# Another order of batch 1's norm beside chunk 0, four transfers on GpSimd's queue, and two sums of w_out elsewhere in chunk 1

## The chip, the core and the metric

The kernel runs on one core of a Trainium2 chip. A core has five engines that run their own instruction queues and wait for one another by semaphores: TensorE (PE, matmuls; PEld is its weight load), VectorE (DVE), ScalarE (ACT), GpSimd (POOL) and SyncE (SP), which here only issues DMA transfers. ScalarE and GpSimd issue transfers too. An engine takes its instructions strictly in order, so that one that waits holds all behind it. The metric is the device time of one execution in microseconds (us), and of several runs the median.

## What is computed

Eight batches of eight heads go through a linear attention with an RMS norm, and the result, seen as 4608 tokens of 512, through a gated feed-forward layer of 1536. All of it is float32; the weights arrive as float64.

```python
def _attn_ref(q, k, v, g_norm):            # q, k, v: (8, 8, 576, 64)
    kv = np.einsum('bhsd,bhse->bhde', k, v)
    out = np.einsum('bhsd,bhde->bhse', q, kv)
    rms = np.sqrt(np.mean(out * out, axis=-1, keepdims=True) + 1e-06)
    return (out / rms * g_norm).astype(np.float32)

def _moe_ref(x, w_gate, w_val, w_out):     # x: (4608, 512), w_gate, w_val: (512, 1536), w_out: (1536, 512)
    gate = 1.0 / (1.0 + np.exp(-(x @ w_gate)))
    val = x @ w_val
    return (gate * val @ w_out).astype(np.float32)
```

## The kernel before

The 4608 tokens are worked in nine chunks of 512. The attention of batch b is put between the matmuls of the chunks ahead of the one that needs it, and its loads further ahead still. Three stretches matter here.

**Chunk 0 (22 to 116 us), first layer.** It is done plainly: eleven blocks of eight matmuls of 512 columns (function `plain`, L599; the profile shows each such matmul as two). A block has a gate (a sigmoid on ScalarE, L604) and an end (a product on VectorE, L607), which are put out beside the next block. Beside each matmul stands a place, numbered 0 to 87, and the string `places` (L807) says which steps are put out there, in which order. Since every engine works in order, this string sets the order of VectorE's and ScalarE's queues. The steps:

- `CV`: the next step of the conversion of the weights from float64 (`convert`, L179). A unit is 128 x 1024 weights; units 0 to 11 are pairs of w_gate and w_val blocks, units 12 to 17 pairs of rows of w_out. It takes five steps on VectorE, L197, L212, L224, L228 and L235 (L237 for w_out), with two of ScalarE between (L202 after the first, L217 after the second). L224 waits for L202, and L228 for L217. When a unit is done its buffer is loaded again, for the unit three further on (L161, L163, on SP). What is left of the steps when the 88 places are over goes beside chunk 0's second layer (L876).
- `a...` and `b...`: the first and second half (`heads_run`, L416) of batch 1's heads: `u` (matmuls, L439), `sq` (square, ScalarE, L444), `s0`, `s1` (reductions, VectorE, L447), `rt` (root, ScalarE, L450, with a load of its function table), `rc` (reciprocal, VectorE, L483), `n0` to `n2` (six scalings each, ScalarE, L479), `x0`, `x1` (two transposes each, VectorE, L462 and L464, and four transfers to xT, SP, L473).
- `t00` to `t11`: transposes of q (VectorE, L408 and L410). `t11` also puts out the twelve loads of batch 2's first q (L119, L120).
- `LL`, `LL2`: the loads of k and v of batches 1 and 2 (`load_late`, L125): eight transfers of 256 KB on SP (L134), and four of 64 KB for the last 64 rows (L139).
- `KV`, `KV2`: the matmuls k times v of batches 1 and 2 (L389, and L396 for the last 64 rows); `C` and `D` copy the results (ScalarE, L404, L405), `ASIDE` sets batch 2's aside (ScalarE, L400).
- `W0`, `W1`: sums of the converted weights on GpSimd (L751).

**Chunk 0, second layer (116 to 158 us).** Twelve rows of w_out in pairs, sixteen matmuls in the profile to a pair (`second`, L833). Pair f needs unit 12 + f/2.

**Chunks 1 to 8.** Both layers go by a scheme with 26 products in place of 32: sums of weights and sums of tokens are multiplied (L957 in the first layer, L1059 in the second), and what comes out is combined on ScalarE (L923) and VectorE (L927). A chunk's first layer has three blocks of 26 products, 0 to 77 in all; its second layer has 26, in the order of `PRODUCTS2` but for a few. GpSimd makes most of the sums of the first layer's results (L733). In chunk 1 the sums of the converted weights are made on the way: of w_gate and w_val, which SP stores for the later chunks (`keep_w1`, L768), and of w_out (`w_form`, L1027). A list at L1151 says which sum of w_out is put out after which product: triples of product, number of the sum, and 1 for GpSimd or 0 for VectorE; `at1` is for the first layer, `at2` counts the products done in the second. Sum 22 (weights 7 and 12) is read by product 10, sum 23 (6 and 14) by product 16. Sum 22 is written over part of the second block's sums of w_gate and w_val, sum 23 over part of the third block's. Both are kept on the core or stored as before.

Behind each second layer stands `load_late` for the batch two chunks on: batch 3's after chunk 1, read at L389 near 282 us.

Of the kernel before, what the change touches and what calls it, by code (L numbers as in the profile page):

```python
# [20 lines left out]
def kernel(  # L21
# [11 lines left out]
    nc = tc.nc  # L33

    B, H, S, HD = q.shape
# [9 lines left out]
    PH = P // 2  # L45
# [19 lines left out]
    GH = G // 2  # L65
# [59 lines left out]
    def load_late(b):  # L125


        if b >= B:
            return
        mains = {}  # L130
        for n in range(NHP):
            for name, src in (("k", k), ("v", v)):
                mains[n, name] = t = kv_place(len(mains))
                nc.sync.dma_start(out=t.rearrange("p (h c) -> p h c", h=2),  # L134
                                  in_=src[b, 2 * n:2 * n + 2, 0:S4].rearrange("h (p j) d -> p h (j d)", j=NK4))
        rest = kv_place(len(mains))
        for i, src in enumerate((k, v)):
            for r in range(2):
                (nc.sync if b == 1 else nc.scalar).dma_start(out=rest[PH * r:PH * r + PH, GH * i:GH * i + GH].rearrange("p (h d) -> p h d", d=HD),  # L139
                                  in_=src[b, NHP * r:NHP * r + NHP, S4:S].rearrange("h p d -> p h d"))  # L140
        kv_late[b] = mains, rest

# [381 lines left out]
    def kv_place(i):  # L524
        return h_more.rearrange("p j s c -> p (j s c)")[:, G * i:G * i + G]
# [256 lines left out]
    def w1_form(c, j, part, v):  # L782
        if c == 1:
# [11 lines left out]
    spare_sg = sgs.pop()  # L795
    batch1, second_batch = feed(1), feed(2)
    named = {"LL": lambda: load_late(1), "LL2": lambda: load_late(2), "KV": batch1[0][0], "KV2": second_batch[0][0],
             "W0": lambda: w1_sums(0), "W1": lambda: w1_sums(1),
             "ASIDE": second_batch[0][2], "CV": convert_step}
# [4 lines left out]
    for i, which in enumerate("ab"):  # L804
# [2 lines left out]
    places = """  # L807
        1:CV,CV 2:CV,Q0 4:CV,CV 5:CV,CV 6:CV,LL 7:CV,CV 10:CV,CV 11:Q1 15:CV 16:CV,CV 17:t00
        18:CV,CV 19:t01 20:KV 22:CV,CV,C 25:CV 26:CV,CV 29:au,LL2 30:CV
        31:asq 32:CV,t10,as0 34:CV,as1,art 35:CV 36:t11,arc,an0 37:an1 38:CV,an2 40:CV,CV 41:CV,ax0  # L810
        43:ax1 44:KV2,ASIDE 46:CV,W0 47:bu 48:CV,CV,bsq 50:CV,bs0 52:CV,CV 54:bs1 55:CV,CV,brt,D 57:CV,CV 58:CV 60:CV,brc
        62:bn0,bn1 63:bn2 64:CV 65:CV,CV,CV 66:CV,CV 67:CV 71:bx0 72:CV 74:W1 75:bx1
        80:CV,CV,CV,CV,CV 84:CV 87:CV,CV
    """
    at_place = {}
    for some in places.split():
        p, names = some.split(":")
# [45 lines left out]
    def x_sum(c, n):  # L863
        if c not in x_ops:
            x_ops[c] = x_sums(c)
        x_ops[c][n]()
# [160 lines left out]
    def w_form(v, eng, at_once=True):  # L1027
        sx_, x, sy, y = next(s_[1:] for s_ in W_SUMS if s_[0] == v)
        if sx_ > 0:
            eng.tensor_tensor(out=W_AT[v], in0=W_AT[x], in1=W_AT[y], op=op_of(sy))  # L1030
        else:
            nc.vector.scalar_tensor_tensor(out=W_AT[v], in0=W_AT[x], scalar=-1.0, in1=W_AT[y], op0=ALU.mult,
                                           op1=op_of(sy))
        if v not in STAY:
            stores.append(lambda: nc.sync.dma_start(out=kept3[STREAM.index(v)].rearrange("p (j n) -> p j n", j=N3),
                                                    in_=W_AT[v]))
            if at_once:
                stores.pop()()

    def second_layer_fast(c, at):  # L1040
# [62 lines left out]
        for i in range(1, NPR):  # L1103
            if i != 3:
# [8 lines left out]
                else:  # L1113
                    product(i, blocks)
                    finish(i)
        load_late(c + 2)

    fill.extend(x_early)
# [13 lines left out]
    for c in range(1, NG):  # L1132
        at1, at2 = {}, {}
        for p, step in x_late:
            at1.setdefault(p, []).append(step)
        x_late = []
        if c + 1 < B:
            kv, first_, then = second_batch if c == 1 else feed(c + 1)
            for p, step in (list(zip((21, 22) if c == 2 else (19, 20), kv)) if c > 1 else []) + first_:
                at1.setdefault(p, []).append(step)  # L1140
            for p, step in zip((3, 6) if c == 1 else (4, 6), then):
                at2.setdefault(p, []).append(step)
        if c + 1 < NG:
            for n, p in enumerate(X1 if c == 1 else X2 if c + 1 < B else X3):
                step = lambda n=n, c=c: x_sum(c + 1, n)
                if p < NPR:
                    at2.setdefault(p, []).append(step)
                else:
                    x_late.append((p - NPR, step))
        if c == 1:  # L1150
            for at_, forms in ((at1, ((28, 9, 0), (30, 10, 0), (34, 12, 0), (52, 11, 1), (57, 14, 0), (58, 8, 1), (61, 19, 0), (64, 16, 1))), (at2, ((1, 13, 0), (2, 22, 0), (3, 23, 1), (4, 25, 1), (9, 15, 0), (10, 24, 0), (10, 20, 0), (11, 17, 0), (12, 18, 0), (13, 21, 0)))):  # L1151
                for p, n, pool_ in forms:
                    at_.setdefault(p, []).append(lambda n=n, eng=nc.gpsimd if pool_ else nc.vector, at_once=at_ is at1 or n == 13: w_form(n, eng, at_once))
        first_layer_fast(c, at1)
        if c == 1:
            sgs += [spare_sg] + more_sgs
        second_layer_fast(c, at2)
# [30 lines left out]
```

## Time and profile before

Three runs: median 1004.05 us (1003.74 to 1005.06). The profiled execution took 1004.44 us, with a span of 1002.7 us from its first to its last instruction.

| engine | busy us | share of the span | instructions |
|---|---|---|---|
| TensorE matmul | 993.8 | 99% | 5958 |
| TensorE weight load | 815.8 | 81% | 5958 |
| VectorE | 722.1 | 72% | 1198 |
| ScalarE | 342.5 | 34% | 606 |
| GpSimd | 617.5 | 62% | 988 |

By stretch, busy us of each engine:

| us | TensorE | VectorE | ScalarE | GpSimd |
|---|---|---|---|---|
| 50 to 75 | 25.00 | 20.20 | 16.43 | 0.00 |
| 75 to 100 | 25.00 | 23.99 | 17.06 | 24.30 |
| 100 to 125 | 24.43 | 24.80 | 9.10 | 24.61 |
| 125 to 150 | 24.84 | 24.57 | 8.49 | 23.74 |
| 230 to 240 | 10.00 | 9.77 | 2.23 | 7.36 |
| 240 to 250 | 10.00 | 9.59 | 1.12 | 9.61 |
| 250 to 260 | 9.67 | 6.79 | 0.00 | 8.24 |
| 300 to 400 | 100.00 | 70.01 | 30.89 | 56.97 |

A line of the timeline gives start and duration in us, the engine, the line of the kernel, the operation, what it writes and reads, how many such instructions in a row, and in brackets how long the engine had been idle before and what ended that. Matmuls are pipelined: each shows longer than the distance to the next one, so that the distance of their starts tells the pace.

### The profile page before, as it was taken

To read this page: it belongs to the slowest core of one execution; us is meant where nothing else is said; L and a number is where in the kernel's file an instruction comes from. 1 tells how busy PE (TensorE), PEld (TensorE's weight loads), DVE (VectorE), ACT (ScalarE), POOL (GpSimd) and SP (SyncE) were. 2 spreads that over 40 slices of the span, in tenths; PEclk is the share of its full clock that TensorE was granted. 3 is DMA by queue.
4 is the path that set the end of the run, shared out by engine and by line. 5 is a ranking of instruction groups with operands and counts; after the bars stand their busy time and mean duration, and the time that the engine had idled before them with its cause. 6 is when DMAs were issued, how large, how long until landed. Compare 5 with 4: busy or idle time off the path is not lost.

```text
span 1002.7 us, 16624 instructions
## 1 busy us (share of the span) xinstructions
PE 993.8 (99%) x5958; PEld 815.8 (81%) x5958; DVE 722.1 (72%) x1198; ACT 342.5 (34%) x606; POOL 617.5 (62%) x988
## 2 busy tenths in 40 slices
PE   8999999999999999999999999999999999999998
PEld 7455447888888888888888888888888888888887
DVE  4989999889757756784677676866587566755672
ACT  4566332562144213530344124421342133213320
POOL 1509997798359633965186707861595449744963
PEclk9999999999999999999999999999999999999999
DMA  9995414673799568846875577755864555444514
GB/s 271 269 265 183 172 51 115 215 236 127 248 301 272 176 189 240 239 156 203 257 240 171 181 223 237 203 171 179 258 201 141 167 173 211 156 149 162 214 53 122
DMA packets 156114, 195.43 MB, mean 195 GB/s; under 512 B 84832, under 2 KB 128864, under 8 KB 156032
## 3 DMA queue, kind: packets, MB, share of 16 engines
q0 software_dynamic: 22000, 114.11, 34.4%
q1 hardware_dynamic: 126864, 78.16, 27.6%
q10 hardware_dynamic: 7168, 2.10, 0.9%
q8 instruction: 47, 0.77, 0.3%
q14 instruction: 35, 0.29, 0.1%
HBM read 160.50 MB, written 25.56 MB: 186 GB/s over the span
## 4 chain that ended last, share of the span: by engine, by line
PE 73%; POOL 2%; DMA 1%; issue 0%; SPq 0%; DVE 0%; POOLq 0%
PE mm L957 46%; PE mm L1059 24%; PE at L439 1%; POOL h L733 1%; PE at L389 1%; DMA h_more<-in_v_dram 1%; POOL w_ring L1030 0%; POOL h_more L733 0%; PE at L396 0%; SPq L134 0%; POOL w L780 0%; DVE sg L927 0%; POOLq L780 0%; POOLq L1030 0%
## 5 line engine op out<-in xcount | busy, mean ns | idle before, releaser
L957 PE MATMUL mm<-xs,w 128*128 128x256 f32 x1428 | 331.8, 380 | 0.0
L957 PEld LDWEIGHTS mm<-xs,w 128*128 128x128 f32 x1428 | 270.5, 190 | 37.1
L957 PE MATMUL mm<-xT,w 128*128 128x256 f32 x948 | 229.8, 380 | 0.0
L957 PEld LDWEIGHTS mm<-xT,w 128*128 128x128 f32 x948 | 179.5, 190 | 25.0 <-issue 0.5
L780 POOL DMA_DIRECT2D w<-kept x84 | 46.8, 557 | 189.4 <-PE mm L957 187.3
L927 DVE TENSOR_TENSOR sg<-sg,mm 128x512 f32<-128x512 f32 (+1 forms) x176 | 100.7, 599 | 85.5 <-PE mm L957 41.5
L1059 PE MATMUL mm<-w,h 128*128 128x256 f32 x630 | 143.1, 379 | 0.3 <-POOL h L733 0.3
L1059 PEld LDWEIGHTS mm<-w,h 128*128 128x128 f32 x630 | 119.6, 190 | 17.0 <-POOL h L733 0.7
L919 POOL TENSOR_TENSOR h<-h,sg 128x512 f32<-128x512 f32 x72 | 96.0, 1350 | 57.0 <-DVE h L927 31.0
L923 ACT COPY temps<-mm 128x512 f32<-128x512 f32 (+1 forms) x128 | 66.0, 538 | 186.9 <-PE mm L1059 94.7
L733 POOL TENSOR_TENSOR h<-h 128x128 f32<-128x128 f32 x216 | 112.1, 531 | 16.6 <-DVE h_more L733 13.1
L1059 PE MATMUL mm<-w,h_more 128*128 128x256 f32 x474 | 108.2, 379 | 0.0
L916 ACT ACTIVATE sg<-sg 128x512 f32<-128x512 f32 x96 | 59.7, 630 | 131.5 <-DVE sg L927 131.5
L1059 PEld LDWEIGHTS mm<-w,h_more 128*128 128x128 f32 x474 | 90.1, 190 | 12.2
L923 ACT COPY sg<-mm 128x512 f32<-128x512 f32 (+1 forms) x112 | 56.9, 510 | 86.5 <-PE mm L1059 45.0
L733 POOL TENSOR_TENSOR h_more<-h 128x128 f32<-128x128 f32 x120 | 61.6, 517 | 34.3 <-DVE h L919 30.0
L927 DVE TENSOR_TENSOR temps<-temps,mm 128x512 f32<-128x512 f32 (+1 forms) x96 | 59.4, 619 | 25.9 <-PE mm L1059 16.6
L599 PE MATMUL mm<-xT,w 128*128 128x512 f32 x176 | 77.8, 596 | 0.1
L927 DVE TENSOR_TENSOR temps<-mm,temps 128x512 f32<-128x512 f32 (+1 forms) x64 | 39.8, 622 | 50.9 <-PE mm L1059 23.6
L923 ACT COPY h<-mm 128x512 f32<-128x512 f32 x48 | 28.1, 585 | 140.4 <-PE mm L957 126.4
L927 DVE TENSOR_TENSOR sg<-mm,sg 128x512 f32<-128x512 f32 (+1 forms) x64 | 39.7, 620 | 45.1 <-PE mm L957 24.5
L599 PEld LDWEIGHTS mm<-xT,w 128*128 128x128 f32 x176 | 32.6, 190 | 39.2 <-issue 36.8
(145 smaller groups left out, 1284.2 us busy)
## 6 DMA issues: line engine op xcount, KB each, us to landing
w<-kept POOLq DMA_DIRECT2D x42, 896.0 KB, 5.7
w<-kept POOLq DMA_DIRECT2D x90, 384.0 KB, 4.6
w<-kept POOLq DMA_DIRECT2D x42, 768.0 KB, 5.5
out_dram<-sg SPq DMA_DIRECT2D x119, 64.0 KB, 1.7
h_more<-in_k_dram SPq DMA_DIRECT2D x28, 256.0 KB, 5.6
h_more<-in_v_dram SPq DMA_DIRECT2D x28, 256.0 KB, 6.5
q<-in_q_dram SPq DMA_DIRECT2D x96, 72.0 KB, 5.0
xT<-xTs SPq DMA_DIRECT2D x96, 72.0 KB, 4.4
```

Of the source, the lines that this page charges most:

```text
L389: nc.tensor.matmul(ps[HD * g:HD * g + HD, m, e], mains[2 * m + g, "k"][:, c], mains[2 * m + g, "v"][:, c], start=(e == 0 and j == 0), stop ...
L439: nc.tensor.matmul(u[HD * e:HD * e + HD, o:o + HD], qTs[HD * g:HD * g + HD, c:c + HD], kvq[HD * g:HD * g + HD, t == NSL, m, e], start=True ...
L599: nc.tensor.matmul(self.ps[i], w[("wg", "wv")[i], self.f][:, m, :], xT[self.c][:, m, :], start=(m == 0), stop=(m == NMT - 1), skip_group_c ...
L733: ops.append((eng, lambda v=v, x=x, sign=sign, y=y, eng=eng: eng.tensor_tensor(out=h_form(v, j), in0=h_form(x, j), in1=h_form(y, j), op=op ...
L780: nc.gpsimd.dma_start(out=granule(g)[:, 0:n], in_=kept1[g // NPA % N3, g % NPA][:, 0:n])
L916: nc.scalar.activation(out=o["o" + step[1]], in_=o["o" + step[1]], func=AF.Sigmoid)
L919: mult.tensor_tensor(out=o[x], in0=o[x], in1=o[y], op=ALU.mult)
L923: nc.scalar.copy(out=o[out_], in_=o[expr])
L927: tt(out=o[out_], in0=o[x], in1=o[y], op=ALU.add if sign == "+" else ALU.subtract)
L957: nc.tensor.matmul(regions[name][1][:, g], ws[:, g], xf[c][wv], start=(new and g == 0), stop=True, skip_group_check=True)
L1059: nc.tensor.matmul(regions[name][1], h_form(hv, j), ws[:, j], start=(used[i] and j == 0), stop=(j == N3 - 1), skip_group_check=True)
```

## The change

Three things are different.

1. The string of places. Batch 1's first half: both reductions and the root now stand at place 32 (they were at 32 and 34), the reciprocal at 34 ahead of a conversion step, `n0` at 34 (36), `n1` at 36 (37), `n2` at 37 (38), and `t11` behind the conversion step at 36 instead of ahead of the reciprocal. Place 36 gets one conversion step more and place 87 has one instead of two, so that between the two each place puts out the step that was put out at the next such place before; ahead of 36 and behind 87 the count is the old one. On VectorE this changes the order of conversion steps, reductions, transposes and ends from about 63 to 120 us; no instruction is added or left out.
2. The four transfers of batch 2's last 64 rows of k and v go to GpSimd's queue. They were on ScalarE's. Batch 1's stay on SP's, those of batches 3 to 7 on ScalarE's.
3. In chunk 1 sum 22 of w_out is made after product 53 of the first layer and no longer after the second finished product of the second layer, on VectorE as before; sum 23 is made at its old place on VectorE, and no longer on GpSimd.

TensorE's instructions and their order are the same. On SP, one load of w_out now comes ahead of eight xT transfers.

```diff
-                (nc.sync if b == 1 else nc.scalar).dma_start(out=rest[PH * r:PH * r + PH, GH * i:GH * i + GH].rearrange("p (h d) -> p h d", d=HD),
+                (nc.sync if b == 1 else nc.gpsimd if b == 2 else nc.scalar).dma_start(out=rest[PH * r:PH * r + PH, GH * i:GH * i + GH].rearrange("p (h d) -> p h d", d=HD),
                                   in_=src[b, NHP * r:NHP * r + NHP, S4:S].rearrange("h p d -> p h d"))
...
-        31:asq 32:CV,t10,as0 34:CV,as1,art 35:CV 36:t11,arc,an0 37:an1 38:CV,an2 40:CV,CV 41:CV,ax0
+        31:asq 32:CV,t10,as0,as1,art 34:arc,CV,an0 35:CV 36:CV,t11,an1 37:an2 38:CV 40:CV,CV 41:CV,ax0
...
-        80:CV,CV,CV,CV,CV 84:CV 87:CV,CV
+        80:CV,CV,CV,CV,CV 84:CV 87:CV
...
-            for at_, forms in ((at1, (..., (52, 11, 1), (57, 14, 0), ...)), (at2, ((1, 13, 0), (2, 22, 0), (3, 23, 1), (4, 25, 1), ...))):
+            for at_, forms in ((at1, (..., (52, 11, 1), (53, 22, 0), (57, 14, 0), ...)), (at2, ((1, 13, 0), (3, 23, 0), (4, 25, 1), ...))):
```

More of the change, by code (lines that the diff above doesn't have):

```diff
@@ L1150 @@
         if c == 1:
-            for at_, forms in ((at1, ((28, 9, 0), (30, 10, 0), (34, 12, 0), (52, 11, 1), (57, 14, 0), (58, 8, 1), (61, 19, 0), (64, 16, 1))), (at2, ((1, 13, 0), (2, 22, 0), (3, 23, 1), (4, 25, 1), (9, 15, 0), (10, 24, 0), (10, 20, 0), (11, 17, 0), (12, 18, 0), (13, 21, 0)))):
+            for at_, forms in ((at1, ((28, 9, 0), (30, 10, 0), (34, 12, 0), (52, 11, 1), (53, 22, 0), (57, 14, 0), (58, 8, 1), (61, 19, 0), (64, 16, 1))), (at2, ((1, 13, 0), (3, 23, 0), (4, 25, 1), (9, 15, 0), (10, 24, 0), (10, 20, 0), (11, 17, 0), (12, 18, 0), (13, 21, 0)))):
                 for p, n, pool_ in forms:
```

## The prediction, made before the changed kernel was run

> **What bounds the kernel now.** I read four views: the page (section 1: TensorE, PE, busy 993.8 of 1002.7 us, granted clock 1.00 throughout), TensorE's waits, its timeline where they fall, and the other engines' timelines just before. The waits after the first 30 us:
>
> ```profile
> PE mm L833 <- DVE w L237: 0.7, 3, 0.4
> ...
> PE mm L1059 <- POOL h L733: 0.3, 1, 0.3
> PE at L389 <- DMA h_more<-in_v_dram: 0.2, 1, 0.2
> ```
>
> These (us in total, times, longest) are net of the modelled overlap of matmuls; the true loss is read from starts:
>
> ```profile
> 97.52 11.32 PE L599 MATMUL mm<-xT,w 128*128 128x512 f32 x26
> 108.68 7.03 PE L599 MATMUL at<-xT,w 128*128 128x512 f32 x16
> 116.06 7.10 PE L833 MATMUL mm<-w,h 128*128 128x512 f32 x16 [0.35 <-DVE w L237]
> 123.38 7.13 PE L833 MATMUL mm<-w,h 128*128 128x512 f32 x16 [0.21 <-DVE w L237]
> 130.67 27.73 PE L833 MATMUL mm<-w,h 128*128 128x512 f32 x64 [0.16 <-DVE w L237]
> ...
> 251.91 1.03 PE L1059 MATMUL mm<-w,h 128*128 128x256 f32 x4
> 253.27 5.88 PE L1059 MATMUL mm<-w,h 128*128 128x256 f32 x26 [0.33 <-POOL h L733]
> ...
> 281.96 1.26 PE L389 MATMUL at<-h_more 128*64 128x64 f32 x34
> 283.44 1.12 PE L389 MATMUL at<-h_more 128*64 128x64 f32 x30 [0.22 <-DMA h_more<-in_v_dram]
> ```
>
> 26 matmuls from 97.52 to 108.68 take 0.429 each, so 16 take 6.87. The next groups start 7.38, 7.32 and 7.29 later: 0.51 + 0.45 + 0.42 = **1.38 us** lost to converted units of w_out that came late. At 253.27 four matmuls of 0.216 (156 in 33.67, chain of waits) would have let the next start at 252.77: 0.50, and 0.1 more for the slower restart (26 in 5.72): **0.6 us**. At 283.44, 34 of 0.032 (64 in 2.02) end at 283.03: **0.41 us**. TensorE's order is the same in both kernels and it works without a gap from 290 to 1000, so all that the change can win is about 2.4 us; what it can lose has no such bound.
>
> **Part 1: batch 1's norm, two units and four transfers.** Why are the units late?
>
> ```profile
> 60.15 2.15 ACTq L139 DMA_DIRECT2D h_more<-in_v_dram  x2
> 62.35 1.13 ACT L444 ACTIVATE sqs<-at 128x1152 f32<-128x1152 f32 x1 [3.08 <-DMA h_more<-in_k_dram]
> ...
> 72.02 1.22 DVE L228 SCALAR_TENSOR_TENSOR cz<-st,cz 128x1024 uint32<-128x1024 uint32 x1 [2.00 <-ACT cz L217]
> ...
> 82.45 0.75 DVE L447 TENSOR_REDUCE ms<-sqs 128x9 f32<-128x576 f32 x1 [0.43 <-ACT sqs L444]
> 83.12 1.28 DVE L235 SCALAR_TENSOR_TENSOR w<-w,g_col,cz 128x1024 f32<-128x1024 f32 x1
> ```
>
> ScalarE's square (asq) waits until its own queue has issued four transfers, at 62.30, though its operand is there when TensorE's L439 ends, 60.24 + 1.38 = 61.62. Later VectorE stands 2.00 for a conversion's L217, queued on ScalarE behind twelve scalings (2.54). From 76 on VectorE hardly rests (24.8 of 25 us from 100 to 125), and a lead gained before is kept until 131.
>
> I replay the new order with the trace's own durations (times in us of this profile). Square 61.62 to 62.75; as0 and as1 (0.67 apiece) to 64.1; L607 64.2 to 64.8; root on ScalarE 64.5 to 64.85, behind its table load; reciprocal to 65.05; L235 1.2, L197 0.6, L212 0.55, both transposes 0.9: 68.3. ScalarE: six scalings (1.41) to 66.5, L202 67.0 to 68.1, L217 to 69.2, twelve scalings to 71.7, table 72.9, sigmoid 73.5. So VectorE: L224 to 69.5, L228 to 70.7, L235 71.9, L197 72.5, x0 73.4; L607 after the sigmoid, 73.5 to 74.1; x1 75.0, L212 75.6, L224 (1.59 beside GpSimd) 77.2. Here a new wait stands: L217 is now queued on ScalarE behind the copy to kv_ahead, which needs TensorE's L396 (77.10): copy to 77.5, L217 to 78.6. Behind it on VectorE wait L228, L607 and L235: 78.6 + 1.2 + 0.6 + 1.2 = 81.6, or 82.5 with L228 and L235 at their slowest (1.74 and 1.63). The reduction at 82.45 is set by TensorE in both kernels. But L235 then stood behind it and now stands ahead: **a lead of 1.19** (the next L197 at 83.12, not 84.31), 1.14 by the slow durations.
>
> Need against supply: without stalls L833's groups start at 115.55, 122.42 and 129.29. The units were ready at 115.92, 123.32 and 130.61 (L237 rows: start plus duration); with the lead 114.7, 122.1 and 129.4. Only the third is late, by 0.1, so the part is worth min(lead, 1.38), less restarts: I take **1.3**, from bounds of 0 (the lead is lost to a wait not seen) and 1.5 (all, with a restart of 0.1). The step that place 36 has more is this L235's and its followers' way forward; at place 87 it is given back, and from there VectorE's order is the old one, but for one L197 of w_out (0.6 to 1.2) ahead of an L607 (0.6): both are done before the next L237 either way.
>
> Four transfers on GpSimd's queue: before, GpSimd is idle from 40.7 to 75.39 (34.70), so nothing is queued behind them but the sums of w1 that start there. They need TensorE's L396 of batch 1 (done 52.4); four issues at 0.6 to 0.7 (its own L119 and L120 rows from 31 to 40) end near 55, and 5.5 to landing (same rows) gives 60.5; they are read at 76.64. Cost nothing, with 16 us of cover; without it, each us of landing after 76.64 would be a us of TensorE's. The Trainium skill speaks against this move: "DMA: Bandwidth & Descriptors", section "SWDGE vs HWDGE vs iDMA", says GpSimd writes such descriptors into SBUF through what VectorE can lock, and "SBUF — State Buffer", section "A bandwidth-pool intuition that's wrong (but worth ruling out)", gives about 3.1 us for a transfer of 0.62 beside such a VectorE copy; by it four would take an estimated 12.4 and land near 70, still in time but with 6 us of cover. The issues from 28 to 41 stayed at 0.55 to 0.74 beside a VectorE over 90% busy, so here the row speaks against the rule. On SP, these four no longer share turns with its loads, which may start some 2 us sooner (between its eight it waited 2.2 for such transfers); VectorE waited for such a load once, 0.2 us: nothing. One w_out transfer goes ahead of eight xT transfers on SP, at about 0.5 apiece; the first xT sum reads them at 148, over 30 us later: nothing.
>
> **Part 2: two sums of w_out.**
>
> ```profile
> 210.59 1.41 DVE L447 TENSOR_REDUCE ms<-sqs 128x9 f32<-128x576 f32 x2 [2.40 <-ACT sqs L444]
> ...
> 237.20 2.53 POOL L1030 TENSOR_TENSOR w_ring<-w,w 128x768 f32<-128x768 f32 x1
> ```
>
> Sum 22 (L1030, 0.97 to 1.97 in its rows) goes into VectorE's 2.40 us gap, right behind the transposes that end at 208.2: free. It overwrites weights that SP was storing: the last such transfer issues at about 205.2 (the last of four kept rows on SP from 202.99 to 205.72), and 2.0 to 2.4 (kept rows of 128 KB) lands it by 207.6, before VectorE comes at 208.2. Sum 23 leaves GpSimd, busy almost without rest from 233.4 to 253.21 (the end of the sum that TensorE waits for at 253.27), and takes on VectorE the 1.2 us that 22 gave up there: VectorE even. GpSimd is 2.53 (or 1.81, its neighbour's) ahead, against a stall of 0.50: the stall goes, **0.6**, bounds 0 and 0.6. Sum 23 is read at 249.32 and done by 239.
>
> **Part 3: the load behind it.** ScalarE's transfer at 258.29 comes right when GpSimd's sum at 257.54 ends; SP's stores then wait 3.3 for such a transfer to land (264.31), and batch 3's loads follow, the last landing at 283.3. GpSimd comes 1.3 to 2.5 earlier and TensorE 0.6, so this chain gains 0.7 or more on TensorE, against 0.41. But the loads share the DMA engines: bounds -1.9 (the second rival) and 0.4, taken **0.3**.
>
> Sum: 1.3 + 0.6 + 0.3 = **2.2 us**. Profiled execution: 1004.44 (span 1002.7 and 1.74 around it) gives 1002.2, span 1000.5; the runs' median lies 0.39 below it: 1004.05 - 2.2 = **1001.8**.
>
> **Rivals.**
> - One half only: the lead is lost before 116 (for: ScalarE loads its table twice around 88 to 92 and VectorE waits 0.43 at 92.25; against: that chain moves with the lead), leaving 0.6, 1003.4; or GpSimd stays late (against: 2.53 is five times the stall), leaving 1.3 to 1.6, 1002.5 to 1002.7.
> - Given back at 283: the batch 3 loads keep their old time and TensorE, 1.9 early, waits 2.3 there: 1004.0. For: the chain of waits puts 7.85 us of one load there. Against: what starts them follows TensorE and GpSimd.
> - Slower: sum 22 stands at the head of VectorE's queue for SP's store of the old weights; both reductions, L1032 and the combining of the third block queue behind it, then TensorE's banks. Its cover is 0.6 to landing, then 0.4 to 1.4 of the gap, then an estimated 0.9 (a bank is filled again a product of four matmuls later at the soonest, 4 x 0.216); it decides from a landing at about 212.7, where 4.5 - 1.4 - 0.9 uses up the 2.2. A landing of 11.1 us (the slowest st load) would be at 216.3: 8.1 late, 5.8 lost, less 2.2: 1007.6. For: SP issues without rest from 199 to 209. Against: kept transfers landed in 2.0 to 4.0.
>
> **Chances.** Forecast 0.62, 1001.4 to 1002.3; one half 0.18; given back 0.08; slower 0.12. Forecast and halves hold 0.80: range 1001.2 (2.5 won and 0.3, the runs' spread below the median) to 1003.6. 0.2% is 2.0 us, about what a measurement of this kernel can tell: faster lies below 1002.04, most of the forecast, 0.55; within 0.33 (0.07 of the forecast, the halves, the given back); slower 0.12.
>
> **What would show it.** Right: asq near 61.6, no 2.0 wait at 72, L833 starting near 115.6 with at most one short gap; L957 of chunk 1 near 156.8; no gap of L1059 after GpSimd; sum 22 between the transposes and the reductions without a wait. Wrong: L833 still waiting three times; VectorE idle before L1030 near 207; L396 near 76 waiting for GpSimd's transfers; a wait of over 0.5 before L389 near 281.

## The result, and the profile after

On the same chip the changed kernel took **1003.12 us** (median of 22 runs, 1001.99 to 1005.6) and the kernel before 1004.97 (22 runs, 1003.64 to 1007.61): a ratio of 0.9982, 95% interval 0.9975 to 0.999, or 1.85 us less. The profiled execution of the changed kernel took 1003.68 us, with a span of 1001.9.

TensorE's order is the same in both, so that its records can be cut at the same instructions. The stretches are the distances of starts: from the last block of L599 (16 matmuls) to chunk 1's first L957, from there to its first L1059, from there to the next L957, batch 3's L389 to the next L957, and from there to the last matmul.

| stretch, us | before | after | difference |
|---|---|---|---|
| start of the last L599 block | 108.68 | 109.67 | +0.99 |
| to chunk 1: second layer of chunk 0 | 49.56 | 48.07 | -1.49 |
| chunk 1, first layer | 70.36 | 71.00 | +0.64 |
| chunk 1, second layer | 34.27 | 33.67 | -0.60 |
| L389 and L396 of batch 3 | 2.92 | 2.41 | -0.51 |
| all behind it | 713.47 | 713.73 | +0.26 |

The first row is what happened before 60 us: here the first loads of v let TensorE wait 1.3 at L301, 1.0 more than before. Nothing of the change stands there; the row lay between 108.1 and 109.7 in twelve of the fourteen profiles of this study (107.9 and 113.2 in the others). The rest adds up to -1.70. TensorE's waits after 60 us in the changed kernel are now one line (us in total, times, longest):

```profile
PE mm L957 <- POOL h L733: 0.4, 1, 0.4
```

All three waits of before are gone, and this one is new. TensorE's timeline of the changed kernel at the places where before it had its gaps:

```profile
109.67 7.03 PE L599 MATMUL at<-xT,w 128*128 128x512 f32 x16
116.53 41.36 PE L833 MATMUL mm<-w,h 128*128 128x512 f32 x96
...
225.50 1.03 PE L957 MATMUL mm<-xs,w 128*128 128x256 f32 x4
226.94 1.10 PE L957 MATMUL mm<-xs,w_ring 128*128 128x256 f32 x4 [0.41 <-POOL h L733]
...
252.05 6.64 PE L1059 MATMUL mm<-w,h 128*128 128x256 f32 x30
...
281.50 2.08 PE L389 MATMUL at<-h_more 128*64 128x64 f32 x64
```

L833 runs in one piece of 96; four and 26 of L1059 have become 30; 34 and 30 of L389 have become 64. But the four matmuls at 225.50 would have let the next start at 226.37 (4 x 0.216); it starts 0.57 later, and 0.07 more is lost in the restart (1.10 for the four in place of 1.03). This is product 76, the last but one of chunk 1's first layer.

What came late for it is read in VectorE's and GpSimd's timelines. First the kernel before:

```profile
205.61 4.13 POOL L919 TENSOR_TENSOR h<-h,sg 128x512 f32<-128x512 f32 x3
210.52 1.82 POOL L1030 TENSOR_TENSOR w<-w 128x768 f32<-128x768 f32 x1
...
211.93 1.23 DVE L1032 SCALAR_TENSOR_TENSOR w<-w,w 128x768 f32<-128x768 f32 x1
...
222.35 2.29 DVE L927 TENSOR_TENSOR sg<-temps 128x512 f32<-128x512 f32 x1
224.74 2.68 DVE L927 TENSOR_TENSOR sg<-sg,mm 128x512 f32<-128x512 f32 x4
```

and the changed kernel:

```profile
205.11 4.84 POOL L919 TENSOR_TENSOR h<-h,sg 128x512 f32<-128x512 f32 x3
210.73 1.82 POOL L1030 TENSOR_TENSOR w<-w 128x768 f32<-128x768 f32 x1
216.72 1.81 POOL L1030 TENSOR_TENSOR w<-w 128x768 f32<-128x768 f32 x1
222.00 2.26 POOL L1030 TENSOR_TENSOR w<-w,w 128x768 f32<-128x768 f32 x1
...
207.62 1.19 DVE L1030 TENSOR_TENSOR w<-w,w 128x768 f32<-128x768 f32 x1
210.09 1.41 DVE L447 TENSOR_REDUCE ms<-sqs 128x9 f32<-128x576 f32 x2 [1.28 <-ACT sqs L444]
211.42 1.95 DVE L1032 SCALAR_TENSOR_TENSOR w<-w,w 128x768 f32<-128x768 f32 x1
...
217.38 1.70 DVE L927 TENSOR_TENSOR h<-h,temps 128x512 f32<-128x512 f32 x1
...
222.51 2.29 DVE L927 TENSOR_TENSOR sg<-temps 128x512 f32<-128x512 f32 x1
224.91 2.68 DVE L927 TENSOR_TENSOR sg<-sg,mm 128x512 f32<-128x512 f32 x4
```

GpSimd's three L1030 here are sums 11, 8 and 16, in this order. TensorE is 0.50 earlier than before, and all else should be. Sum 22 (L1030 on VectorE) starts at 207.62 without a wait, and the reductions still find their gap: 210.09 is 210.59 less 0.50. But GpSimd's three L919 take 4.84 in place of 4.13, since the third takes 1.99 where it took 1.27 (single records of the group). So GpSimd's next sum, sum 11, comes at 210.73, not at 210.02, and ends at 212.55. VectorE's L1032 (sum 14), which before ran behind the greater part of it, begins at 211.42, and takes 1.95 in place of 1.23. Behind it VectorE is 0.70 later against TensorE than before.

That lateness is not simply carried on. By 217.38 VectorE has won part of it back and is 0.44 late. But the L927 there runs beside GpSimd's sum 8, which is 0.70 late, and ends 0.55 after it in both kernels (219.08 after 218.53, before 218.88 after 218.33): VectorE is 0.70 late again. The L927 at 222.51 runs beside sum 16 and ends 0.54 after it (224.80 after 224.26; before 224.64 after 224.09). So it takes 2.29 in both kernels, and ends 0.66 later against TensorE since sum 16 does.

The four L927 behind it free banks, that is, parts of PSUM that TensorE's next products write into. The third of them, by its single record, ended at 226.63 before and ends at 226.79 now, and product 76 starts 0.15 after it: before there was a margin of 226.87 - 226.63 - 0.15 = 0.09 us, and 0.66 - 0.09 is the 0.57 that TensorE loses. The bracket names a GpSimd L733 as the releaser; that is inferred from what ended last, and the experiments below speak against it. In the run with sum 14 moved to product 60, where the bracket names L927, product 76 starts the same 0.15 after the third of them.

### The profile page after: what moved, and what is told of

Read it like the earlier page. It is cut to its first block, busy times and chain, and to the rows that moved or that the text cites. A ratio compares the mean times of both kernels' runs of the same rounds, so it can differ in the third digit from the quotient of the medians.

```text
span 1001.9 us, 16623 instructions
## 1 busy us (share of the span) xinstructions
PE 993.2 (99%) x5958; PEld 815.9 (81%) x5958; DVE 723.3 (72%) x1199; ACT 342.2 (34%) x606; POOL 617.8 (62%) x991
## 4 chain that ended last, share of the span: by engine, by line
PE 94%; POOL 2%; DMA 1%; ACT 1%; SPq 1%; issue 1%; DVE 1%; POOLq 0%; ACTq 0%; DVEq 0%
PE mm L957 51%; PE mm L1059 27%; PE mm L599 8%; PE mm L833 4%; PE at L439 2%; PE at L389 1%; DMA v<-in_v_dram 1%; PE at L599 1%; POOL h_more L733 1%; POOL h L733 1%; POOL h L919 0%; POOL w L1030 0%; SPq L93 0%; PE at L396 0%; DVE sg L927 0%
## 5 line engine op out<-in xcount | busy, mean ns | idle before, releaser
L957 PE MATMUL mm<-xs,w 128*128 128x256 f32 x1428 | 331.9, 380 | 0.0
L957 PEld LDWEIGHTS mm<-xs,w 128*128 128x128 f32 x1428 | 270.4, 190 | 37.4 <-DVE sg L927 0.4
L957 PE MATMUL mm<-xT,w 128*128 128x256 f32 x948 | 229.8, 380 | 0.0
L957 PEld LDWEIGHTS mm<-xT,w 128*128 128x128 f32 x948 | 179.5, 190 | 25.0 <-issue 0.2
L927 DVE TENSOR_TENSOR sg<-sg,mm 128x512 f32<-128x512 f32 (+1 forms) x176 | 100.8, 600 | 85.0 <-PE mm L957 40.3
L1059 PE MATMUL mm<-w,h 128*128 128x256 f32 x630 | 142.8, 379 | 0.0
L1059 PEld LDWEIGHTS mm<-w,h 128*128 128x128 f32 x630 | 119.7, 190 | 16.3
L919 POOL TENSOR_TENSOR h<-h,sg 128x512 f32<-128x512 f32 x72 | 96.7, 1360 | 56.4 <-DVE h L927 30.4
L733 POOL TENSOR_TENSOR h<-h 128x128 f32<-128x128 f32 x216 | 113.1, 535 | 16.5 <-DVE h_more L733 13.1
L1059 PE MATMUL mm<-w,h_more 128*128 128x256 f32 x474 | 108.2, 379 | 0.0
L1059 PEld LDWEIGHTS mm<-w,h_more 128*128 128x128 f32 x474 | 90.1, 190 | 12.2
L733 POOL TENSOR_TENSOR h_more<-h 128x128 f32<-128x128 f32 x120 | 61.6, 517 | 35.0 <-DVE h L919 30.8
L927 DVE TENSOR_TENSOR temps<-temps,mm 128x512 f32<-128x512 f32 (+1 forms) x96 | 59.4, 619 | 25.7 <-PE mm L1059 16.5
L599 PE MATMUL mm<-xT,w 128*128 128x512 f32 x176 | 77.8, 596 | 0.1
L927 DVE TENSOR_TENSOR temps<-mm,temps 128x512 f32<-128x512 f32 (+1 forms) x64 | 39.8, 622 | 50.7 <-PE mm L1059 24.3
L927 DVE TENSOR_TENSOR sg<-mm,sg 128x512 f32<-128x512 f32 (+1 forms) x64 | 39.7, 620 | 46.7 <-PE mm L957 24.7
L599 PEld LDWEIGHTS mm<-xT,w 128*128 128x128 f32 x176 | 32.6, 190 | 39.2 <-issue 36.1
```

Source lines behind the costliest of these rows:

```text
L599: nc.tensor.matmul(self.ps[i], w[("wg", "wv")[i], self.f][:, m, :], xT[self.c][:, m, :], start=(m == 0), stop=(m == NMT - 1), skip_group_c ...
L733: ops.append((eng, lambda v=v, x=x, sign=sign, y=y, eng=eng: eng.tensor_tensor(out=h_form(v, j), in0=h_form(x, j), in1=h_form(y, j), op=op ...
L919: mult.tensor_tensor(out=o[x], in0=o[x], in1=o[y], op=ALU.mult)
L927: tt(out=o[out_], in0=o[x], in1=o[y], op=ALU.add if sign == "+" else ALU.subtract)
L957: nc.tensor.matmul(regions[name][1][:, g], ws[:, g], xf[c][wv], start=(new and g == 0), stop=True, skip_group_check=True)
L1059: nc.tensor.matmul(regions[name][1], h_form(hv, j), ws[:, j], start=(used[i] and j == 0), stop=(j == N3 - 1), skip_group_check=True)
```

## The experiments

Each ran beside runs of the kernel before on the same chip; the experiments of one chip share these (24, 28 or 35 runs). Times in us; the stretches are those of the table above; "start" is its first row.

| run | start | second layer of chunk 0 | chunk 1, first | chunk 1, second | L389, L396 | behind | median (runs) | ratio, 95% |
|---|---|---|---|---|---|---|---|---|
| e1_places_queue | 109.46 | 48.07 | 70.36 | 34.26 | 3.66 | 714.30 | 1003.22 (10) | 0.9982, 0.9971 to 0.9994 |
| e2_sums_only | 108.51 | 50.23 | 71.01 | 33.67 | 2.41 | 713.47 | 1004.42 (10) | 0.9991, 0.9982 to 1.0 |
| e3_22_back | 108.23 | 48.07 | 70.36 | 33.67 | 2.42 | 713.47 | 1002.05 (5) | 0.9964, 0.9951 to 0.9977 |
| e6_14_later | 108.17 | 48.07 | 71.35 | 33.67 | 2.41 | 713.71 | 1003.19 (8) | 0.9979, 0.9964 to 0.9994 |
| e4_no_queue | 107.90 | 48.07 | 71.00 | 33.67 | 2.41 | 713.47 | 1002.81 (10) | 0.9977, 0.9964 to 0.9991 |
| e5_queue_only | 108.55 | 50.22 | 70.36 | 34.27 | 2.41 | 713.47 | 1005.49 (10) | 1.0003, 0.9994 to 1.0012 |
| e3_again | 108.65 | 48.07 | 70.36 | 33.67 | 2.98 | 713.47 | 1002.3 (6) | 0.9972, 0.996 to 0.9984 |
| e7_14_earlier | 108.15 | 48.07 | 70.36 | 33.67 | 2.41 | 714.50 | 1002.38 (10) | 0.9977, 0.9968 to 0.9986 |
| e8_before_again | 108.92 | 50.24 | 70.36 | 34.28 | 3.40 | 713.47 | 1004.54 (10) | 0.9995, 0.998 to 1.001 |
| e9_after_again | 108.61 | 48.07 | 71.01 | 33.67 | 2.41 | 714.81 | 1003.04 (12) | 0.9972, 0.9959 to 0.9986 |
| e10_22_back_no_queue | 113.24 | 48.07 | 70.36 | 33.67 | 3.02 | 713.47 | 1002.53 (12) | 0.997, 0.9956 to 0.9984 |
| e11_16_later | 108.40 | 48.07 | 70.36 | 33.67 | 2.41 | 713.77 | 1002.23 (10) | 0.9964, 0.9952 to 0.9977 |

**The parts alone.** The first has only the new places and the four transfers on GpSimd's queue, the second only the two sums.

> Part 1 alone: the new places and batch 2's four transfers on GpSimd, sums 22 and 23 as before. The changed kernel waits 0.65 us at product 76 of chunk 1's first layer. Theory A (sum 22): made after product 53 it holds GpSimd's products by 0.7 us, GpSimd's sum 11 then lies across VectorE's sum 14, and VectorE combines 0.7 late; so here no wait at product 76, none before L833, but 0.6 before L1059 for GpSimd; 1.5 us under the kernel before, ratio 0.9985. Theory B (pace): TensorE, early by part 1, catches VectorE whatever the sums; so 0.4 to 0.65 is lost at product 76 here too, and the ratio is 0.9990.

> Part 2 alone: sums 22 and 23 as in the changed kernel, places and queues as before. Theory A: 0.4 to 0.6 us lost at product 76, nothing in L1059, nothing at batch 3's L389, and the three waits of 1.4 us before L833 stay: 0.5 us under the kernel before, ratio 0.9995. Theory B: no wait at product 76, 1.0 us under, ratio 0.9990.

The new wait stands where the sums are moved (71.01) and not where the places are (70.36): it belongs to part 2. So does the end of the wait at L1059 (33.67 against 34.26). The whole of L833's loss goes with the places. With the old places and the sums moved, e2 lost even more there (50.23, with two waits and not the three expected) than the kernel before in its profile (49.56). In e1, L389 waited longer than before, 3.66 - 2.41 = 1.25, and another L389, at 707, 0.82 more.

**Sum 22 back, sum 23 on VectorE.** The edit, on the changed kernel:

```diff
-(at1, (..., (52, 11, 1), (53, 22, 0), (57, 14, 0), ...)), (at2, ((1, 13, 0), (3, 23, 0), ...))
+(at1, (..., (52, 11, 1), (57, 14, 0), ...)), (at2, ((1, 13, 0), (2, 22, 0), (3, 23, 0), ...))
```

> The changed kernel with sum 22 back after the second finished product of the second layer, sum 23 still on VectorE. Theory A: no wait at product 76; VectorE has 1.2 us more from 236 to 240, which holds GpSimd by as much, of its 2.5 gained; so no wait in L1059, or one under 0.3; 2.3 to 2.5 us under the kernel before, ratio 0.9976. Theory B: the 0.65 at product 76 stays, ratio 0.9982 as in the changed kernel.

The new wait is gone, and the wait at L1059 has not come back: sum 23 alone, taken from GpSimd, is worth the whole 0.60. After 60 us TensorE waits nowhere in this profile. The move of sum 22, which costs 0.64 us, bought nothing.

**Sum 14 out of GpSimd's way.** In the changed kernel sum 14 moves from product 57 to 60 (`(57, 14, 0)` becomes `(60, 14, 0)`), behind sum 11's end.

> The changed kernel with sum 14 made after product 60 and not 57, so clear of GpSimd's sum 11. Theory A: VectorE's sum takes 1.0 to 1.2 us and not 1.95, the combining comes 0.7 sooner, no wait at product 76; 2.4 us under the kernel before, ratio 0.9976. Theory B, or if only the work of sum 22 counts: 0.4 to 0.65 still lost there, ratio 0.9982.

What was expected of theory A failed: the first layer is 71.35, worse. VectorE's and TensorE's timelines of this run:

```profile
210.47 0.69 DVE L927 TENSOR_TENSOR sg<-sg,mm 128x512 f32<-128x512 f32 x1 [0.46 <-PE mm L957]
...
212.80 0.95 DVE L1032 SCALAR_TENSOR_TENSOR w<-w,w 128x768 f32<-128x768 f32 x1
213.67 1.21 DVE L1032 SCALAR_TENSOR_TENSOR w<-w 128x768 f32<-128x768 f32 x1
...
225.79 1.10 PE L957 MATMUL mm<-xs,w_ring 128*128 128x256 f32 x4 [0.75 <-DVE sg L927]
```

Sum 14 does take 0.95 when it is away from sum 11. But the time in front of 210.47, in which VectorE waits for other engines anyway (0.46, and 0.17 and 0.18 at the next two), now goes unused, and sum 14's 0.95 falls where VectorE has none to spare. GpSimd's sums hold it here too: the L927 at 220.75, beside sum 16, takes 2.04, so that this run doesn't part the two. Here the bracket names L927, VectorE's, as the releaser.

**Sum 14 earlier** (`(54, 14, 0)`), right behind sum 22:

> The changed kernel with sum 14 (L1032) at place 54, right behind sum 22, and no longer at 57. Theory A (sum 22 holds GpSimd by 0.7, GpSimd's next sum, L1030, is then late and lies across VectorE's L1032, 1.95 in place of 1.23, and VectorE's combining comes 0.66 late to product 76): L1032 now falls into what is left of VectorE's gap (1.28 us), beside GpSimd's L919; it takes 0.95 to 1.25, GpSimd's L919 group grows to about 5.5, the combining behind it only reads PSUM and is not held, and the wait before product 76 goes: first layer of chunk 1 70.36 to 70.5. Theory C (VectorE simply has no room for 1.2 us more in this stretch): the wait stays at 0.6 to 0.7, first layer 71.0. Should L1032 have to wait here for SP's store of the old weights, VectorE idles before it, the reductions start after 210.1 less the shift of the start, and the first layer is over 71.0.

The wait is gone (70.36), as theory A expected, but not for the durations it named:

```profile
206.10 1.21 DVE L1030 TENSOR_TENSOR w<-w,w 128x768 f32<-128x768 f32 x1
207.23 2.02 DVE L1032 SCALAR_TENSOR_TENSOR w<-w,w 128x768 f32<-128x768 f32 x1
...
215.41 2.10 DVE L927 TENSOR_TENSOR h<-h,temps 128x512 f32<-128x512 f32 x1
...
220.52 0.94 DVE L927 TENSOR_TENSOR sg<-temps 128x512 f32<-128x512 f32 x1
221.56 2.68 DVE L927 TENSOR_TENSOR sg<-sg,mm 128x512 f32<-128x512 f32 x4
```

L1032 took 2.02, not 0.95 to 1.25, and GpSimd's L919 stayed at 4.84. It cost nothing, since most of it lay in VectorE's gap and the rest in its waits behind that; at 215.41 VectorE is as early against TensorE as in the kernel before. The L927 there, beside sum 8, takes 2.10 and makes it 0.65 late, though sum 14 is out of sum 11's way. But VectorE wins 0.45 of this back, where the kernel before waits 0.44 for a copy of ScalarE's (at 219.92). In the changed kernel that copy ends 0.42 late, since the reciprocal (L485) is 0.52 late behind sum 14 and ScalarE's scalings wait for it. So sum 14's hold has a part in the loss, by way of ScalarE. The L927 that took 2.29 in both kernels takes 0.94 here, because it now comes ahead of sum 16: it starts 0.47 earlier against TensorE than in the changed kernel, and sum 16 comes 0.39 later.

**Sum 16 later.** That last line suggested a sharper test: leave sums 22 and 14 as in the change, and move only GpSimd's sum 16, `(64, 16, 1)` to `(66, 16, 1)`.

> The changed kernel with sum 16, GpSimd's (L1030, 2.26 us from 222.00), put out after product 66 in place of 64; sum 22 stays after 53. In both kernels VectorE's L927 of 2.29 us at 222.51, by its neighbours some 0.7 to 0.95 long, lies wholly beside that sum. Theory A (what makes VectorE late at product 76 is not its work but being held by GpSimd's sums, sum 11 across L1032 and sum 16 across this L927): this L927 takes about 0.94, the four that free the banks start 0.6 to 1.3 earlier, and the wait before product 76 goes although L1032 still takes 1.95: first layer 70.36. Theory C (VectorE has 1.2 us too much work in the stretch): the wait stays at 0.5 to 0.7, first layer 70.9 to 71.0. GpSimd's own L733 sums behind the moved one may come late for L1059 near 229; then the second layer is over 33.67.

```profile
206.36 1.19 DVE L1030 TENSOR_TENSOR w<-w,w 128x768 f32<-128x768 f32 x1
210.14 1.95 DVE L1032 SCALAR_TENSOR_TENSOR w<-w,w 128x768 f32<-128x768 f32 x1
...
221.24 0.94 DVE L927 TENSOR_TENSOR sg<-temps 128x512 f32<-128x512 f32 x1
222.28 2.67 DVE L927 TENSOR_TENSOR sg<-sg,mm 128x512 f32<-128x512 f32 x4
...
222.98 1.83 POOL L1030 TENSOR_TENSOR w<-w,w 128x768 f32<-128x768 f32 x1
```

The three L733 whose end the changed kernel's bracket named as what ended the wait, end at 225.63 in this run, behind product 76, which starts at 225.09: they release nothing there. VectorE does the same work as in the changed kernel, sum 22 in its new place and sum 14 held to 1.95. With sum 16 (222.98) behind it, L927 takes 0.94 in place of 2.29, and the wait is gone. The start of that L927 is as late against TensorE as in the changed kernel, and only its hold is gone. So it is not that VectorE lacks 1.2 us of room (theory C): without sum 16's hold, which the kernel before has too, the lateness would have cost nothing. That the move of sum 16 cost nothing at L1059 is seen in the 33.67.

**The queue.** The changed kernel with the four transfers back on ScalarE's queue, and the kernel before with only these moved to GpSimd's:

> The changed kernel with batch 2's four transfers back on ScalarE's queue: is the new order of places alone worth the 1.49 us that the stretch from the last block of L599 to chunk 1's L957 lost (49.56 before, 48.07 after)? In the changed kernel ScalarE's square starts at once; here it must stand behind the four issues again, some 0.7 us later (62.35 before, 62.65 less 0.98 of a later start after). Theory Q (the prediction's replay: square first, so every step behind it moves, and the queue is part of the lead): the lead falls by 0.7, the third pair and a part of the second come late again, L833 waits once or twice, and the stretch is 48.5 to 48.9. Theory W (VectorE's wait of 1.40 us before L228 near 79.6, which TensorE's L396 sets through ScalarE's copy, swallows the 0.7): that wait is 0.6 to 0.8 in place of 1.40, everything behind it keeps its time, no wait before L833, the stretch 48.07. By both: first layer of chunk 1 71.0, second 33.67.

> The kernel before with batch 2's four transfers on GpSimd's queue and nothing else: what are the transfers worth by themselves? Theory Q (the square 0.7 earlier hands its 0.7 on): VectorE's wait near 72 for ScalarE's L217 is about 1.3 in place of 2.0, the lead 0.7, and the stretch from the last L599 block to chunk 1's L957 some 48.8 to 49.1 in place of 49.56, with L833 waiting less. Theory W (the old order of places holds it up elsewhere, behind the twelve scalings or behind TensorE): the square is earlier, but the stretch stays 49.4 to 49.7 and L833 waits three times, so that the gain of part 1 is the order's, not the queue's. By both: first layer of chunk 1 70.36, L1059 still waits 0.6 (second layer 34.27).

Without the queue the stretch is 48.07 all the same; with the queue alone it is 50.22. Why, is seen in the run without it:

```profile
61.09 1.13 ACT L444 ACTIVATE sqs<-at 128x1152 f32<-128x1152 f32 x1 [2.74 <-PE at L439]
...
77.84 1.23 DVE L228 SCALAR_TENSOR_TENSOR cz<-st,cz 128x1024 uint32<-128x1024 uint32 x1 [1.20 <-ACT cz L217]
```

From the start of the last L599 block the square is 0.21 later than in the changed kernel (61.09 - 107.90 against 62.65 - 109.67), not the 0.69 of the kernel before; and VectorE's wait before L228, which TensorE's L396 ends through ScalarE's copy and L217, is 1.20 in place of 1.40. The wait swallows what the square loses. That is theory W's mechanism, but on less than either theory assumed: 0.21 and not 0.7. In e10, also without the queue, ScalarE's issues were done before the square's operand was there, and the square was not late at all. That the wait, with 1.20 left, would also swallow the 0.7 is argued and not shown. In the kernel with the queue alone the square was 0.68 earlier than in the kernel before. VectorE still stood 2.02 before L228 near 71, since the twelve scalings and L217 behind them moved along, and was 0.52 earlier there. But it lost this at 78.49, where L224 waits 0.79 for ScalarE's L202, queued behind the copy that needs TensorE's L396; and the reduction at 82.32, which TensorE's L439 sets through the square, starts when it did before. So the gain of part 1 is the order's, as theory W has it, though the 50.22 lies outside its 49.4 to 49.7.

**Both kernels again.** The kernel before and the changed kernel, for a second profile; and the kernel before with the new places and sum 23 on VectorE alone.

> The kernel before, once more, for its trace: its order of the places lost 1.38 us before L833 in its own profile, but the two other kernels with that order (sums alone, queue alone) lost 2.04 there, with one L235 of 1.76 to 1.82 us in place of 1.28 near 83. Theory S (the loss depends on how VectorE's instructions happen to fall beside GpSimd's, so it differs between executions of one program): the stretch from the last L599 block to chunk 1's L957 is 49.5 or 50.2, whichever, and part 1 is worth 1.4 to 2.1 in the times. Theory T (the other two edits reach back into chunk 0 somehow): 49.5 to 49.6 again. By both: first layer of chunk 1 70.36, second 34.27; L389's wait near 282 anything from 0 to 1, since it stood at 0.4, 1.15 and 0 in the three kernels with GpSimd's old order. Time: ratio 1.000, within 0.001.

> The changed kernel once more, beside the version of the next run on the same chip. Its wait before product 76 is 0.65 again if it is made by the order of the instructions, as in the two other kernels that have both sum 22 at product 53 and sum 14 at 57 (first layer of chunk 1 71.0), and is 0 if it was an accident of one execution. No wait before L833, second layer 33.67. Ratio 0.998.

> The kernel before with the new order of places and sum 23 on VectorE alone: sum 22 at its old place, batch 2's four transfers on ScalarE's queue. If the queue is worth nothing (as the run without it and the run of it alone say), it does what the changed kernel with sum 22 back did: stretches 48.07, 70.36 and 33.67, ratio 0.9964 to 0.9974, 0.5 to 1.0 us under the changed kernel on the same chip. If the queue does help in an order that leaves VectorE less work near 60 us, L833 waits once (48.2 to 48.6).

TensorE's waits after 60 us in the second profile of the kernel before:

```profile
PE mm L833 <- DVE w L237: 1.2, 2, 1.0
PE at L389 <- DMA h_more<-in_v_dram: 0.7, 1, 0.7
PE mm L1059 <- POOL h L733: 0.3, 1, 0.3
```

The stretch before chunk 1 is 50.24, as in the two other kernels with the old places, and not 49.56: of four profiles of that order, the one that the prediction was made from lost the least, 1.49 against 2.15 to 2.17 over 48.07. Most of the difference is in VectorE's L235 near 83, 1.76 us in this profile and 1.28 in the first, and 1.76 and 1.82 in the two other kernels; it comes right behind the reduction that TensorE sets. Why it differs is open. The new wait of the changed kernel came again, to 0.01 us. Sum 22 back without the queue has none of the four waits but a short one at L389; its last L599 block starts 3.6 us or more later than in any other profile, with a wait of 3.3 at L355 where the kernel before waited 1.1.

**Once more for its time.** Sum 22 back, with the queue:

> The changed kernel with sum 22 back behind the second finished product of the second layer and sum 23 on VectorE, once more, for its time: the profile of its first run showed none of the four stalls. If that holds, it is 2.2 to 2.7 us under the kernel before (1.49 + 0.60 + 0.51 = 2.60 by the stretches), a ratio of 0.9974 to 0.9978, and 0.5 to 0.9 under the changed kernel; if the first run was a fortunate one and the small start-up differences decide, about 1.9, like the changed kernel.

2.8 us under the kernel before, a little more than expected, with a wait of 0.57 at L389 in its profile. The lowest ratio is 0.9964, of e3's first run (5 runs) and of e11 (10 runs). On e11's chip its runs lay between 1001.62 and 1002.4, and the changed kernel's between 1002.29 and 1005.57, medians 1002.23 and 1003.04; the intervals of the ratios still overlap (0.9952 to 0.9977, 0.9959 to 0.9986).

## Why the prediction was right, and where it was not

The forecast was 1001.8 us, a gain of 2.2; measured were 1003.12 and a gain of 1.85. 0.9 of the distance is the kernel before, which took 1004.97 here and 1004.05 in the runs shown ahead of the change. The rest is in the terms, and that the total came near is in part luck: what part 2 missed (0.64) was made up in good part by parts 1 and 3, which gave 0.19 and 0.21 more than forecast. Against any of the other three profiles of the old order, part 1 would have given 2.15 to 2.17.

**Part 1, forecast 1.3, measured 1.49.** The replay held: less the start's 0.99, the square stands at 61.66 (61.62 forecast), the wait before L228 ends at 78.61 (78.6), L833 starts at 115.54 (115.6) and chunk 1 at 156.75 (156.8). All three units came in time, where the third was forecast 0.1 late: the L237 of the units end at 114.13, 121.56 and 128.83 by that clock, 0.54 to 0.57 ahead of the forecast. "A lead gained before is kept until 131" is therefore not strict; it grew from about 1.1 near 84 to 1.8 at 114. The 1.49 is the 1.38 of the prediction's sum and 0.11 of slower restarts behind the waits. The four profiles of the old order show the same the other way: 1.49 or 2.17 lost by one program. The price of the wait was right for the profile at hand, and low for the kernel. And the queue, the first step of the replay, was no part of it: the stretch is 48.07 in all ten profiles with the new places, two of them without the queue, and the queue with the old places gave nothing. GpSimd's four issues took 0.62 each, from 53.66 on, and landed after 3.6 to 4.8, so the 3.1 apiece that the prediction weighed did not come; beside them VectorE ran L224, L228 and L235.

The Trainium skill ("SBUF — State Buffer", section "Who interferes with whom") has an exception that fits: it infers that a `tensor_tensor` takes only the read side of what VectorE and GpSimd share, and that writing descriptors needs the write side. It says this of `tensor_tensor` alone; here the `scalar_tensor_tensor` L228, also with two SBUF inputs, took 1.20 beside the issues, and an issue 0.62.

**Part 2, forecast 0.6, measured -0.04.** This is the step that failed: "Sum 22 ... goes into VectorE's 2.40 us gap, right behind the transposes that end at 208.2: free", with "bounds 0 and 0.6" for the part. GpSimd's half was right: the stall at L1059 went, 0.60. Sum 22 did find the gap, and had no wait for SP's store, so that the slower rival did not come. But the gap was VectorE's only: GpSimd worked there, and was held 0.72 by the sum. That put its sums 11, 8 and 16 0.7 later, each of them held VectorE, and VectorE, at a margin of 0.09 us, came 0.57 late to product 76. The prediction looked for what would be queued behind sum 22, and not for what runs beside it on GpSimd, although it used L224 at "1.59 beside GpSimd" in part 1. The run with sum 22 back shows that all of the loss hangs on it, the run with sum 16 moved that the hold by sum 16 is needed for it. How much of the 0.66 each of the earlier holds gave is read from the timelines and was not tested one by one.

The Trainium skill states this rule, and the prediction did not use it ("SBUF — State Buffer", "Who interferes with whom"): a VectorE instruction with two SBUF inputs and a GpSimd one that reads SBUF exclude each other, the later one waiting for the whole of the other, and a VectorE instruction with one SBUF input, outside its two-port modes, is not touched. The trace agrees in the main: the L927 of 222.51 with two inputs in SBUF ends 0.54 after sum 16 does (224.80 and 224.26) and L1032 0.82 after sum 11 (213.37 and 212.55), a little less than the 0.69 of that L927's neighbour and the 0.95 that L1032 takes away from sum 11, while the L927 that read a PSUM bank stayed at 0.67 to 0.69 beside GpSimd's L733.

**Part 3, forecast 0.3, measured 0.51 here, and not settled in general.** The loads started earlier (268.71 before, 267.49 after, the last 275.45 and 272.24), TensorE did not wait. But over all profiles this wait changes: 0.51, 1.25, 0 and 0.99 in the four with sum 23 on GpSimd, 0 in eight of ten and 0.57 and 0.61 in two with it on VectorE. With GpSimd ahead it is rarer, as the chain of the prediction has it, but neither always gone there nor always present without, and fourteen profiles don't settle its size. Other L389 waited now and then too (at 491 in e7, at 707 in e1 and 705 in e9, 0.8 to 1.1 each). The rival "given back at 283" came in neither profile of the changed kernel, and no profile has its 2.3 there; but a wait of up to 1.25 comes in some executions.

The row "behind" holds +0.26, a stop at 738.96 before an L957 whose weight load waits for an L927. It stood in five of the seven profiles with sum 22 after product 53, and in none of the seven without; why a sum of chunk 1 should matter there stays open.

Summed by its terms, the change was to give 1.3 + 0.6 + 0.3 = 2.2 and gave 1.49 - 0.04 + 0.51 - 0.26 = 1.70 in the profile, and 1.85 in the medians.

## What to carry to other kernels

Here a gap in VectorE's queue was not free, because GpSimd worked beside it and the two held each other: before a sum is put into VectorE's gap, read what GpSimd does in the same microseconds, and follow what is pushed back there to the next place where the two meet. Where an engine frees TensorE's banks, work out its margin first; here it was 0.09 us, less than any one hold, because sum 16 held an L927 for 1.35 in the kernel before already. Moving sum 16 gave that margin back. And a stall of a microsecond should be read from two profiles of a program before it becomes a term, since one program gave 1.49 and 2.17.

## What the runs showed of the hardware

- One sum of 1.19 us on VectorE made GpSimd's L919 beside it 1.99 long in place of 1.27, and a GpSimd sum of 1.82 made VectorE's L1032 1.95 long, against 0.95 alone.
- The same L927 took 2.29 us behind the start of a GpSimd sum and 0.94 ahead of it: two products' difference in where that sum was put out moved VectorE by 1.35.
- Chunk 1's first layer took 70.36 in nine of the fourteen profiles and 71.00 or 71.01 in the four with sums 22, 14 and 16 as in the change, while the stretch of L833 took 49.56 once and 50.22 to 50.24 three times with one order. Both losses thus took few distinct values.
